# Query and key weights in eight transfers instead of two, and two input tiles loaded from ScalarE's queue

## The chip, the core and the metric

The kernel runs on one core of a Trainium2 chip. The metric is the device time of one execution in microseconds (us), as the median of several runs. Engines are named as in the profile: PE is TensorE (PEld its weight loads), DVE is VectorE, ACT is ScalarE, POOL is GpSimd, SP is SyncE, which here only issues DMAs; a name with a q (SPq, ACTq) is the engine's queue of instructions that issue or wait.

## What is computed

```python
x  = layernorm(A_x)                        # 2048 tokens x 512, bf16 (A_x: the input)
s  = mixer(x, wqkv, wo)                    # 32 heads of 16; each token attends to 8 keys, 2 apart, backwards
h  = gelu(layernorm(x) @ w1)               # 512 x 512
x1 = x + shifted(h) @ w2                   # four column groups, shifted by -1, +1, -2, +2 tokens
g  = silu(x1 + gelu(layernorm(x1) @ w3) @ w4)   # 512 x 1376, 1376 x 512
out = x + s * g
```

`mixer` takes queries, keys and values as `x @ wqkv` (512 x 1536), a softmax over the 8 keys, and ends with `@ wo`. The first thing that TensorE needs is therefore a normalised tile of x and the query part of `wqkv`.

## The kernel before

Even and odd tokens are kept apart (`p` is 0 or 1, 1024 tokens each), so that the stride of 2 becomes a band. Tokens are worked on in four chunks `c` of 512, each of four tiles `j` of 128 tokens; chunk 0 and 1 are the even tokens. x lies in `xn[p]` with tokens on partitions; `load_x` fetches it, one tile (128 KB) a transfer in chunk 0, two tiles (256 KB) in the others. `wqk_sb` holds the first 1024 columns of `wqkv`, four row blocks `dt` of 128: columns 0 to 511 are the queries (`k` 0), 512 to 1023 the keys (`k` 1).

All loads at the start are issued by SP (L118, L128, L132), in this order: x tile 0, x tile 1, the query weights (one transfer of 512 KB), x tile 2, x tile 3, the key weights (512 KB), then chunk 1 and chunk 2 (two transfers each), `w1`, and chunk 3 (two).

The work of chunk 0, from L430 on, tile by tile: `stats` (DVE, L208 and L209: mean and variance), `root` (ACT, L217: the square root of the variance), `inverse` (DVE, L220: the reciprocal), `norm` (DVE, L224: subtract and multiply in place). Tiles 0 and 1 go first; `first_columns` then transposes them on PE (L290), and the two halves of the result are copied to `xnT` by DVE (L292) and ACT (L293). Then come tiles 2 and 3 in the same way. `qk(0, 0)` (L309) multiplies the first 256 tokens by the eight blocks `nt` of `wqk_sb`: `nt` 0 to 3 are queries, 4 to 7 keys, four matmuls (`dt`) each. Within it, before `nt` 6 and `nt` 7, tiles 2 and 3 are transposed by `columns` (L264), for `qk(0, 1)` after it.

Each engine executes its instructions in the order of the source: the last lines of the kernel chain each engine's instructions one behind the other. Between engines, the framework places semaphores. In the built program, every DMA that SP or ACT issues signals its landing on one of eight semaphores, taken in turn: the DMAs are numbered in the order in which the program lists them, and SP's and ACT's count in one sequence. A DMA that takes a semaphore which an earlier one used waits, on its own queue, until that one has landed. The listing of the built program is one sequence over all engines, in the order in which the framework's scheduler dispatched them; it knows the order on each engine, not these semaphores. Its first loads stand in it so (work of POOL and PE left out):

```
SP   x tile 0            signals H0
SP   x tile 1            signals H1
SP   wqk_sb (queries)    signals H2
SP   x tile 2            signals H3
SP   x tile 3            signals H4
SP   wqk_sb (keys)       signals H5
SP   chunk 1, tiles 0,1  signals H6
SP   chunk 1, tiles 2,3  signals H7
SP   chunk 2, tiles 0,1  waits H0, signals H0
SP   chunk 2, tiles 2,3  waits H1, signals H1
DVE  stats (0,0)         waits H0
SP   w1_sb               waits H2, signals H2
DVE  stats (0,1)         waits H1
ACT  root (0,0)
ACT  root (0,1)
DVE  norm (0,0), inverse (0,1), norm (0,1)
SP   chunk 3, tiles 0,1  waits H3, signals H3
DVE  copy to xnT (L292)
SP   chunk 3, tiles 2,3  waits H4, signals H4
...
SP   store to row_dram (L249, chunk 0)  waits H5, signals H5
...
SP   store of tile 7 (last lines)       signals H5
ACT  store of tile 7, second half       signals H6
SP   store of tile 7, first half        signals H7
```

The functions that the diff touches, with the line numbers of the profile:

Of the kernel before, what the change touches and what calls it, by code (L numbers as in the profile page):

```python
# [15 lines left out]
def kernel(  # L16
# [13 lines left out]
    pe, dve, act, pool, sp = nc.tensor, nc.vector, nc.scalar, nc.gpsimd, nc.sync  # L30
    P = 128
    S = 2048
    D = 512
# [4 lines left out]
    ND = D // P  # L38
# [6 lines left out]
    TPC = CH // P  # L45
# [16 lines left out]
    xv = A_x.flatten_outer_dims().rearrange("(m two) d -> two m d", two=2)  # L62
# [16 lines left out]
    def bigt(shape, name):  # L79
        return big.tile(shape, BF16, name=name, tag="big")  # L80

    def midt(shape, name):
        return mid.tile(shape, BF16, name=name, tag="s11")

    def smt(shape, name):
        return sm4.tile(shape, BF16, name=name, tag="s4")
# [25 lines left out]
    xn = [bigt([P, M // P, D], f"xn{p}") for p in range(2)]  # L112
    wqkv_v = A_wqkv.rearrange("(dt q) n -> q dt n", q=P)

    def load_x(c, n):
        p, k = c // 2, c % 2
        for t0 in range(k * TPC, (k + 1) * TPC, n):
            sp.dma_start(  # L118
                out=xn[p][:, t0 : t0 + n, :],
                in_=xv[p, t0 * P : (t0 + n) * P, :].rearrange("(i q) d -> q i d", q=P),  # L120
            )
            yield

    wqk_sb = midt([P, ND, 2 * D], "wqk_sb")
    first = load_x(0, 1)
    for k in range(2):
        next(first), next(first)
        sp.dma_start(out=wqk_sb[:, :, k * D : (k + 1) * D], in_=wqkv_v[:, :, k * D : (k + 1) * D])  # L128
    list(load_x(1, 2))
    list(load_x(2, 2))  # L130
    w1_sb = smt([P, ND, D], "w1_sb")
    sp.dma_start(out=w1_sb, in_=B_w1.rearrange("(dt q) n -> q dt n", q=P))  # L132
    list(load_x(3, 2))

    act.preload_act_table_set("sqrt_and_others")
    ident = const.tile([P, P], BF16, name="ident")
# [17 lines left out]
    for e in range(2):  # L154
        dve.tensor_reduce(
            out=sel[:, e : e + 1], in_=ident.rearrange("p (r f) -> p r f", f=2 * DH)[:, :, DH * e : DH * e + DH],
# [43 lines left out]
    def x_tile(c, j):  # L200
        return xn[c // 2][:, (c % 2) * TPC + j, :]

    def stats(c, j, key="l1"):
        if (key, c) not in mvs:
            mvs[key, c] = small.tile([P, TPC, nc.vector.BN_AGGR_DIM], F32, name=key + "m", tag=key + "m")
            rs[key, c] = small.tile([P, TPC], F32, name=key + "r", tag=key + "r")
        st = small.tile([P, nc.vector.BN_STATS_DIM], F32, name=key + "s", tag=key + "s")
        dve.bn_stats(out=st, in_=x_tile(c, j))  # L208
        dve.bn_aggr(out=mvs[key, c][:, j, :], in_=st)  # L209
# [6 lines left out]
    def root(c, a, b):  # L216
        act.activation(rs["l1", c][:, a:b], mvs["l1", c][:, a:b, 1], AF.Sqrt, bias=eps[:, 0:1])  # L217

    def inverse(c, a, b):
        dve.reciprocal(out=rs["l1", c][:, a:b], in_=rs["l1", c][:, a:b])  # L220

    def norm(c, j, key="l1", dst=None):
        x = x_tile(c, j)
        dve.tensor_scalar(  # L224
            out=x if dst is None else dst, in0=x, scalar1=mvs[key, c][:, j, 0:1], scalar2=rs[key, c][:, j : j + 1],
            op0=ALU.subtract, op1=ALU.mult,
        )
# [201 lines left out]

    stats(0, 0)  # L430
    root(0, 0, 1)
    stats(0, 1)
    root(0, 1, 2)
    for j in range(2):
        inverse(0, j, j + 1)
        norm(0, j)
# [52 lines left out]
    for j in range(TPC):  # L489
# [12 lines left out]
        out=w4_sb[:, 0 : NF - 1, :],  # L502
        in_=B_w4[0 : (NF - 1) * P, :].rearrange("(ft q) n -> q ft n", q=P),
# [364 lines left out]
    for n in range(NN - 1):  # L868
# [56 lines left out]
        if n - 1 in final_at and n % 2 == 0 and n < NN - 3:  # L925
            p, i = final_at[n - 1]
# [88 lines left out]
```

## Time and profile before

| | |
|---|---|
| time, median of 3 runs | 198.19 us (197.81 to 198.98) |
| the profiled execution's own time | 197.92 us |
| its span, first to last instruction | 195.9 us |
| PE busy | 189.5 us (97%) |
| DVE, ACT, POOL busy | 124.1 us, 126.7 us, 62.9 us |
| mean granted TensorE clock | 0.998 |
| first matmul of `qk(0, 0)` | 6.73 us from the span's start |
| DMA traffic, first three of 40 slices (4.9 us each) | 149, 330, 270 GB/s |

The span is what the profile shows from the first to the last instruction; 2.0 us of the execution's time lie outside it. The times of instructions are counted from the span's start. A busy share is an average over the whole span; what a change at the start is worth must be read from the first ten microseconds.

### The profile page before, as it was taken

The page shows a single profiled execution, that of the slowest core. Times are in us where ns is not written, and L with a number is a line of the kernel's source. Part 1 is how long each engine was busy: PE and PEld are TensorE (multiplying, and loading weights), DVE is VectorE, ACT ScalarE, POOL GpSimd, SP SyncE. Part 2 cuts the span into 40 slices and gives each one's busy share as a digit, 9 for nine tenths or more (in the row PEclk, how much of TensorE's full clock was granted, in tenths as well). Part 3 has the DMA queues.
Part 4 walks back from the last instruction along what each step waited for, and adds up shares of the span by engine and source line. Part 5 has one row for each costly group of instructions (what it writes and reads, how often), then busy time and mean ns, then how long its engine had stood idle before and what let it go on. Part 6 is the DMA issues. An engine that isn't in the chain of part 4 may idle for free.

```text
span 195.9 us, 6180 instructions
## 1 busy us (share of the span) xinstructions
PE 189.5 (97%) x2607; PEld 100.7 (51%) x2607; DVE 124.1 (63%) x247; ACT 126.7 (65%) x140; POOL 62.9 (32%) x114
## 2 busy tenths in 40 slices
PE   7799999999999999999999999999999999999992
PEld 2688748644444444444445555555555545546551
DVE  4879885029359968200005677788778888886893
ACT  3579867836721534666558788887666666677971
POOL 4146738201301121100000623032625242469761
PEclk9999999999999999999999999999999999999999
DMA  5985265799660366350420012222233271723243
GB/s 149 330 270 137 77 144 161 141 300 357 185 155 3 107 157 162 113 107 0 155 84 0 14 25 65 76 48 67 44 97 67 56 210 27 234 39 87 70 141 109
DMA packets 36251, 23.36 MB, mean 119 GB/s; under 512 B 19680, under 2 KB 35712, under 8 KB 36224
## 3 DMA queue, kind: packets, MB, share of 16 engines
q1 hardware_dynamic: 34864, 22.11, 40.2%
q0 software_dynamic: 1216, 0.81, 2.1%
q8 instruction: 20, 0.33, 0.7%
q10 hardware_dynamic: 144, 0.07, 0.1%
q14 instruction: 7, 0.06, 0.1%
HBM read 12.41 MB, written 5.36 MB: 91 GB/s over the span
## 4 chain that ended last, share of the span: by engine, by line
PE 90%; DVE 4%; ACT 2%; DMA 1%; issue 1%; DVEq 0%
PE w_ps L542 19%; PE w_ps L406 18%; PE qk_ps L309 14%; PE v_ps L595 8%; PE w_ps L342 7%; PE w_ps L366 7%; PE wo_ps L815 5%; PE o_ps L663 5%; PE s_ps L616 3%; PE w_ps L422 1%; DMA xn<-in_A_x_dram 1%; ACT prob L627 1%; DVE prob L636 1%; PE tr_ps L264 1%; PE dt_ps L716 1%
## 5 line engine op out<-in xcount | busy, mean ns | idle before, releaser
L627 ACT ACTIVATE prob<-s_ps 128x2048 bf16<-128x2048 f32 (+1 forms) x18 | 31.9, 1780 | 17.9 <-PE s_ps L616 17.9
L542 PE MATMUL w_ps<-w_sb,h3T 128*128 128x512 bf16 (+1 forms) x176 | 40.8, 380 | 0.0
L410 ACT ACTIVATE h3T<-w_ps 128x1024 bf16<-128x1024 f32 x20 | 20.5, 1023 | 24.9 <-PE w_ps L406 24.9
L706 POOL DMA_DIRECT2D oT<-orw x38 | 19.4, 518 | 49.8 <-DVE orw L671 30.3
L406 PE MATMUL w_ps<-x1nT,w_sb 128*128 128x512 bf16 x160 | 35.0, 379 | 0.0
L309 PE MATMUL qk_ps<-xnT,wqk_sb 128*128 128x256 bf16 (+1 forms) x224 | 29.7, 288 | 0.5 <-DVE xnT L292 0.4
L542 PEld LDWEIGHTS <-h3T 128*128 128x128 bf16 (+1 forms) x176 | 17.0, 98 | 20.4
L309 PEld LDWEIGHTS <-wqk_sb 128*128 128x128 bf16 x224 | 21.5, 98 | 7.6 <-issue 0.8
L406 PEld LDWEIGHTS <-w_sb 128*128 128x128 bf16 x160 | 15.6, 98 | 19.1 <-issue 0.4
L636 DVE TENSOR_TENSOR prob<-prob,band 128x2048 bf16<-128x2048 bf16 (+1 forms) x18 | 21.3, 1183 | 2.4 <-ACT prob L627 2.3
L316 ACT ACTIVATE qT<-qk_ps,sel 128x1024 bf16<-128x1024 f32 x16 | 16.8, 1111 | 7.1 <-PE qk_ps L309 7.0
L831 POOL TENSOR_TENSOR xo<-sg,xo 128x512 bf16<-128x512 bf16 x9 | 11.7, 1305 | 21.6 <-DVE sg L826 21.6
L371 DVE TENSOR_TENSOR xn<-w_ps,xn 128x1024 bf16<-128x1024 f32 x8 | 9.7, 1212 | 13.2 <-PE w_ps L366 13.2
L815 PE MATMUL wo_ps<-wo_sb,oT 128*128 128x512 bf16 (+1 forms) x68 | 16.6, 367 | 0.1
L595 PE MATMUL v_ps<-wv_sb,xnT 128*128 128x512 bf16 x64 | 16.6, 382 | 0.0
L550 DVE TENSOR_TENSOR xn<-w_ps,xn 128x512 bf16<-128x512 f32 x15 | 10.4, 690 | 7.5 <-PE w_ps L542 7.5
L598 DVE CAST v_aug<-v_ps 128x512 bf16<-128x512 f32 x1 | 0.7, 691 | 22.5 <-ACT h3T L410 22.5
L681 ACT ACTIVATE orw<-o_ps 128x896 bf16<-128x896 f32 x16 | 14.6, 913 | 0.4 <-PE dt_ps L716 0.4
L366 PE MATMUL w_ps<-w_sb,hT 128*128 128x512 bf16 x64 | 14.3, 379 | 0.0
L342 PE MATMUL w_ps<-xn2T,w_sb 128*128 128x512 bf16 x64 | 14.3, 379 | 0.0
L213 POOL TENSOR_SCALAR l3r<-l3m 128x4 f32<-128x4 f32 x4 | 1.8, 451 | 36.9 <-DVE l3m L209 36.9
L663 PE MATMUL o_ps<-prob,v_aug 64*32 64x64 bf16 x1088 | 12.2, 196 | 0.3 <-DVE prob L636 0.2
(100 smaller groups left out, 240.1 us busy)
## 6 DMA issues: line engine op xcount, KB each, us to landing
x1n_dram<-xn SPq DMA_DIRECT2D x4, 512.0 KB
xn<-in_A_x_dram SPq DMA_DIRECT2D x6, 256.0 KB
xo<-in_A_x_dram SPq DMA_DIRECT2D x6, 256.0 KB
out_dram<-xo SPq DMA_DIRECT2D x6, 256.0 KB
orw<-rden_d SPq DMA_DIRECT2D x6, 240.0 KB
w_sb<-in_B_w_dram SPq DMA_DIRECT2D x1, 1376.0 KB
w_sb<-in_B_w_dram SPq DMA_DIRECT2D x1, 1280.0 KB
wqk_sb<-in_A_wqkv_dram SPq DMA_DIRECT2D x2, 512.0 KB
```

Source lines behind the costliest of these rows:

```text
L309: pe.matmul(pt[:, b, :], lhsT=wqk_sb[:, dt, nt * P : (nt + 1) * P], rhs=xnT[p][:, dt, ms], start=(dt == 0), stop=(dt == ND - 1),)
L342: pe.matmul(pt[:, b, :], lhsT=w1_sb[:, dt, g * P : (g + 1) * P], rhs=xn2T[:, dt, :], start=(dt == 0), stop=(dt == ND - 1),)
L366: pe.matmul(pt[:, j, :], lhsT=w2_src(p, g, m0), rhs=w2_sb[:, g, :], start=(g == 0), stop=(g == ND - 1),)
L406: pe.matmul(pt[:, b, :], lhsT=w3_sb[:, dt, ft * P : (ft + 1) * P], rhs=x1nT[:, dt, :], start=(dt == 0), stop=(dt == ND - 1),)
L410: act.activation(h3_tile(c)[:, 2 * a : 2 * a + 2, :], pt, AF.Gelu_apprx_tanh)
L542: pe.matmul(pt, lhsT=h3[c][:fs, ft, jj * P : (jj + 1) * P], rhs=w4_sb[:fs, ft, :], start=(ft == 0), stop=(ft == NF - 1 and t < NN - 2),)
L595: pe.matmul(vp, lhsT=xnT[p][:, dt, k0 : k0 + P], rhs=wv_sb[:, dt, :], start=first, stop=last)
L627: act.activation(pr[:, rs_], t[:, rs_], AF.Exp, scale=SCALE)
L636: dve.tensor_tensor(out=w, in0=w, in1=b.unsqueeze(1).to_broadcast([P, m, KB]), op=ALU.min)
L663: pe.matmul(op[32 * cg : 32 * cg + 32, s, g * KB : (g + 1) * KB], lhsT=va[KB * s : KB * s + KB, dt * 8 + h, :], rhs=pr[KB * s : KB * s + K ...
L706: queues[hh % len(queues)].dma_start(out=oT[p][DH * hh : DH * (hh + 1), :, q0 : q0 + nq], in_=w[32 * cg : 32 * cg + DH, ND * jj : ND * jj ...
L815: pe.matmul(pt, lhsT=oT[p][:, dt, i * P : (i + 1) * P], rhs=wo_sb[:, dt, cs], start=(dt == 0), stop=(dt == ND - 1),)
```

## The change

The two transfers of `wqk_sb` become eight, one for each half `k` and row block `dt`: 128 rows of 512 columns, 128 KB each. They follow x tiles 0 and 1 directly on SP's queue. x tiles 2 and 3 leave SP's queue: ACT issues them, the one behind `root(0, 0)`, the other behind `root(0, 1)`. The order of SP's other loads stays. The number of transfers at the start goes from 13 to 19. `load_x` becomes a plain function with a queue as argument.

```diff
-    def load_x(c, n):
-        p, k = c // 2, c % 2
-        for t0 in range(k * TPC, (k + 1) * TPC, n):
-            sp.dma_start(...)
-            yield
+    def load_x(c, j, n=1, queue=sp):
+        p, t0 = c // 2, c % 2 * TPC + j
+        queue.dma_start(
+            out=xn[p][:, t0 : t0 + n, :], in_=xv[p, t0 * P : (t0 + n) * P, :].rearrange("(i q) d -> q i d", q=P)
+        )
 
     wqk_sb = midt([P, ND, 2 * D], "wqk_sb")
-    first = load_x(0, 1)
+    for j in range(2):
+        load_x(0, j)
     for k in range(2):
-        next(first), next(first)
-        sp.dma_start(out=wqk_sb[:, :, k * D : (k + 1) * D], in_=wqkv_v[:, :, k * D : (k + 1) * D])
-    list(load_x(1, 2))
-    list(load_x(2, 2))
+        for dt in range(ND):
+            sp.dma_start(out=wqk_sb[:, dt, k * D : (k + 1) * D], in_=wqkv_v[:, dt, k * D : (k + 1) * D])
+    for c in (1, 2):
+        for j in (0, 2):
+            load_x(c, j, 2)
     w1_sb = smt([P, ND, D], "w1_sb")
     sp.dma_start(out=w1_sb, in_=B_w1.rearrange("(dt q) n -> q dt n", q=P))
-    list(load_x(3, 2))
+    for j in (0, 2):
+        load_x(3, j, 2)
...
     stats(0, 0)
     root(0, 0, 1)
+    load_x(0, 2, 1, act)
     stats(0, 1)
     root(0, 1, 2)
+    load_x(0, 3, 1, act)
     for j in range(2):
         inverse(0, j, j + 1)
         norm(0, j)
     first_columns()
```

More of the change, by code (lines that the diff above doesn't have):

```diff
@@ L113 @@
     wqkv_v = A_wqkv.rearrange("(dt q) n -> q dt n", q=P)
-    def load_x(c, n):
-        p, k = c // 2, c % 2
-        for t0 in range(k * TPC, (k + 1) * TPC, n):
[L118 to L121, printed above, removed]
-            yield
+    def load_x(c, j, n=1, queue=sp):
[3 more added lines that the diff above has]
+        )
     wqk_sb = midt([P, ND, 2 * D], "wqk_sb")
-    first = load_x(0, 1)
+    for j in range(2):
+        load_x(0, j)
     for k in range(2):
-        next(first), next(first)
-        sp.dma_start(out=wqk_sb[:, :, k * D : (k + 1) * D], in_=wqkv_v[:, :, k * D : (k + 1) * D])
-    list(load_x(1, 2))
-    list(load_x(2, 2))
+        for dt in range(ND):
[3 more added lines that the diff above has]
+            load_x(c, j, 2)
     w1_sb = smt([P, ND, D], "w1_sb")
     sp.dma_start(out=w1_sb, in_=B_w1.rearrange("(dt q) n -> q dt n", q=P))
-    list(load_x(3, 2))
+    for j in (0, 2):
+        load_x(3, j, 2)
     act.preload_act_table_set("sqrt_and_others")
```

## The prediction

> **What bounds the kernel now.** The page first: PE is busy for 189.5 of 195.9 us, and the chain that ended last is 90% PE.
>
> ```profile
> PE 90%; DVE 4%; ACT 2%; DMA 1%; issue 1%; DVEq 0%
> ```
>
> So whatever moves the first matmul moves the end by as much: behind it PE works without a pause that a late start could fill. The change touches the first 10 us only, so I read the chain there in order of time (start, length, what).
>
> ```profile
> 0.80 2.33 DMA xn<-in_A_x_dram
> ...
> 3.15 0.70 DVE l1s L208
> ...
> 4.06 0.59 DVE l1s L208
> ...
> 5.46 0.43 DVE xn L224
> ...
> 5.93 0.30 PE tr_ps L290 x2
> ...
> 6.25 0.44 DVE xnT L292
> ...
> 6.73 2.94 PE qk_ps L309 x24
> ```
>
> x tile 0 lands, DVE takes the statistics of tiles 0 and 1, normalises both, PE transposes, DVE copies, and at 6.73 the first `qk` matmul starts. Neither the weights nor x tiles 2 and 3 are on this chain. The waits of the first 30 us show what the weights do cost:
>
> ```profile
> PEld L309 <- DMA wqk_sb<-in_A_wqkv_dram: 0.2, 1, 0.2
> ```
>
> One wait, that of `nt` 4 for the keys (landed at 8.58 by the trace's landing events). In matmul starts it is less: matmul 17 starts 0.195 us behind matmul 16, where the others keep 0.109. The loss is 0.09 us. That is all that earlier weights can win on PE.
>
> ACT's timeline shows the place of the two roots, and that ACT has room around them:
>
> ```profile
> 4.10 0.29 ACT L217 ACTIVATE l1r<-l1m,eps 128x1 f32<-128x1 f32 x1 [2.02 <-DVE l1m L209]
> 4.89 0.29 ACT L217 ACTIVATE l1r<-l1m,eps 128x1 f32<-128x1 f32 x1 [0.50 <-DVE l1r L220]
> 6.37 0.60 ACT L293 ACTIVATE xnT<-tr_ps 128x512 bf16<-128x512 bf16 x1 [1.18 <-PE tr_ps L290]
> ```
>
> The second root is as good as on the chain: it ends at 5.18, its reciprocal starts at 5.26 beside the end of the first norm, and `norm(0, 1)` at 5.46 needs both. If the root is late, all is late after 0.03 us.
>
> Last, SP's waits in the first 15 us:
>
> ```profile
> SPq L249 <- DMA wqk_sb<-in_A_wqkv_dram: 0.5, 1, 0.5
> ```
>
> The store of L249 reads `r2t` and has nothing to do with `wqk_sb`. It is the 14th DMA, the key weights are the 6th: fourteen less eight. This is the ring of eight semaphores at work, and it does hold a queue. `w1` (the 11th) says the same: the 3rd landed at 5.771, `w1` was issued at 5.788.
>
> **The change, part by part.** *Eight pieces on SP.* Issues stand in SP's timeline:
>
> ```profile
> 0.80 0.88 SPq L118 DMA_DIRECT2D xn<-in_A_x_dram  x2
> 1.72 0.43 SPq L128 DMA_DIRECT2D wqk_sb<-in_A_wqkv_dram  x1
> 2.19 0.98 SPq L118 DMA_DIRECT2D xn<-in_A_x_dram  x2
> 3.21 0.43 SPq L128 DMA_DIRECT2D wqk_sb<-in_A_wqkv_dram  x1
> ```
>
> The first seven starts are 0.45 to 0.55 us apart, whatever the size; I take 0.48. The pieces then start at 1.72, 2.20, 2.68, 3.16 (queries) and 3.64, 4.12, 4.60, 5.08 (keys), and chunk 1 at 5.56 instead of 3.69. A 128 KB transfer with nothing ahead of it landed 2.33 and 2.24 us after its issue (x tiles 0 and 1); one behind a 512 KB transfer took 3.9 (tile 2). At 128 KB each 0.48 us (273 GB/s) the pieces stay below the 330 GB/s of the page's second slice, so nothing piles up: 2.2, between 2.0 and 2.4. The queries are there at 5.36, before 6.73; the last keys at 7.28, before the 8.54 at which `nt` 4 is due. Gain 0.09. Chunk 1, 1.9 us later, is needed at 9.36 and would land by 8.6 (2.2, 0.4 for its second 128 KB, 0.4 for what ACT adds); SP's other loads have microseconds to spare, and SP ends its loads near 10, before L249 at 12.29.
>
> The Trainium skill, "DMA: Bandwidth & Descriptors", under "Rules for kernel authors", advises against such cuts: many small transfers should be made one large one. By its fit in "Anatomy of one DMA" (2.0 us and bytes over 436 GB/s, given for another path) a piece takes an estimated 2.3 us, and the sum below would grow by 0.1.
>
> *Two issues on ACT.* The only DMA that ACT issues in the trace:
>
> ```profile
> 192.90 0.39 ACTq L857 DMA_DIRECT2D out_dram<-slots  x1
> ```
>
> If ACT's first issue starts when the first root ends (4.39) and takes 0.39 to 0.51 (SP's rows), it ends between 4.78 and 4.90: 0 to 0.05 us on the second root. The other one lies in the idle time before L293.
>
> *The wait that these issues bring.* This is the costly part. x tile 2 takes a semaphore of the ring, and which one depends on how many DMAs are listed ahead of it. In the listing of before, `w1` stands before `root(0, 0)`, and the first load of chunk 3 behind `root(0, 1)`. With two loads taken out of SP's order ahead of them, both stand earlier if anything. So 15 DMAs are ahead of x tile 2 (two tiles, eight pieces, four of chunks 1 and 2, `w1`), perhaps 16. As the 16th it waits for the 8th to land, the second piece of the keys; as the 17th for the 9th, the third piece. x tile 3 as the 18th waits for the 10th, the last piece. No data are involved.
>
> The 8th is issued at 4.12 and lands at 6.32. ACT executes in order, so behind its wait stand `root(0, 1)`, x tile 3 and L293; for the root waits DVE (`inverse(0, 1)`, `norm(0, 1)`), for that PE. The second root then starts at 6.32 + 0.02 (as `w1` behind its release) + 0.41 (issue) + 0.04 (gap) = 6.79 instead of 4.89: 1.90, less the slack of 0.03, is **1.87 us** on the chain.
>
> x tile 3 may issue at 7.28 and ends at 7.7; L293, now due at 8.24, isn't held. But the tiles come late: tile 2, issued at 6.34, shares the DMA engines with the 256 KB loads of chunks 1 and 2; between 2.3 (alone) and 3.9 (behind 512 KB) I take 2.6, so 8.9 and for tile 3 9.9. DVE wants tile 3 at 7.41 + 1.87 = 9.28 and needs 1.89 us from there to the end of its norm (7.41 to 9.30): 11.8. PE wants it at 10.06 + 1.8 = 11.9, and tile 2, whose norm ends 1.37 after tile 3 is taken, at 9.40 + 1.8 = 11.2 against 11.3. Cost 0 to 0.5; I take **0.2**.
>
> Sum: 1.87 + 0.2 - 0.09 = 1.98 us. Against the profiled execution (197.92) that is 199.90, against the median (198.19; the profile lies 0.27 below) 200.17. Forecast 200.0. With the low value of each term (pieces 0.45 apart, landing in 2.0, issue 0.39, tiles in time) the cost is 1.4; as the 17th, with 0.50, 2.4, 0.51 and 0.5, it is 3.2. So 199.4 to 201.2 for this case.
>
> **The rivals.** *No wait decides: not slower.* If the ring doesn't hold ACT's queue, or x tile 2 is the 12th DMA or earlier, its predecessor has landed by 4.4 and ACT issues between the roots. Then tile 2 lands at 6.7 to 6.9, 0.1 to 0.3 after DVE asks (6.59), which PE doesn't feel: the norm of tile 2 ends at 8.78, its transposes start at 9.40. What stays is the 0.09: 198.1. For it: no ACT issue in this trace waits on the ring. Against it: the listing gives ACT's last DMA its number between two of SP's.
>
> *A shorter wait.* If SP's pieces are dispatched slower than I read from the listing, x tile 2 is the 13th to 15th and waits for a landing at 4.88, 5.36 or 5.84: 0.4 to 1.4 us, 198.6 to 199.6. Against it: the scheduler put `w1`, with 2.5 MB of loads ahead of it, before the root, and now there are 2.25 MB ahead.
>
> *The clock falls.* Between the warm-up matmuls, which end at 4.8, and `qk`, now at 8.6, PE has only eight transposes, 0.9 us in all; before, the pause was 1.9 us. In this trace the matmuls of L147 are 0.427 us apart until 3.65 and 0.217 from 4.0, so a cold PE takes twice the time. Warming took 2.9 us here; so much `qk` work at half speed adds some 1.5 us: 201.5. The Trainium skill, "TensorE: Matmul & The Clock Gate", "The HAM clock gate", says that the half rate returns after an idle window of about 3.4 us that runs freely; no pause here is that long and empty, and the trace has no drop at 1.9.
>
> **How the numbers follow.** The long wait 0.70; no wait 0.14; a shorter wait 0.08; the clock 0.07; rest 0.01. About 0.5% (1 us) is what a measurement of this kernel can tell. Faster by more than that needs a mechanism that I don't see: 0.01. Same: no wait and half of the shorter waits, 0.18. Slower: the rest, 0.81. The range 198.1 to 201.2 holds nearly all of the long and shorter waits and some of no wait.
>
> **What would show it.** In the changed kernel's ACT timeline `root(0, 1)` starts near 6.8, with an ACTq issue right ahead of it that starts within 0.05 us of the landing of a key piece; the first `qk` matmul at 8.6; DVE's wait for the late tiles 0 to 0.6 us; no wait for `wqk_sb`; the first chunk 1 issue near 5.6. Wrong if ACT issues x tile 2 at 4.4, or if the second root stays at 4.9.

## The result and the profile after

The changed kernel takes 206.1 us (median of 6 runs, 204.87 to 208.15), the kernel before 198.29 us: a ratio of 1.037 (95% interval 1.032 to 1.042). The ratios, here and below, leave out single slow runs, over 1.5% above the fastest of their kernel (208.15 here, 202.91 in wait_alone, 207.39 in keep_warm), which medians and ranges still contain: the medians differ by 7.8 us, the ratio stands for 7.3. The forecast was 200.0 us, in a range of 199.4 to 201.2: the sign was right, the size about four times too small. The profiled execution took 204.87 us, its span is 202.9 us; against the 195.9 us of before that is 7.0.

The page's share of the chain that ended last, by engine, and its line on the granted clock:

```profile
PEclk9889999999999999999999999999999999999999
...
PE 72%; DMA 12%; DVE 5%; ACT 3%; SPq 3%; issue 2%; ACTq 0%; DVEq 0%
```

PE has fallen from 90% to 72%, DMA risen from 1% to 12%, and the clock has a dent in the second and third slice. The waits of the first 30 us (engine and line, what was waited for, total, times, longest):

```profile
DVE l1s L208 <- DMA xn<-in_A_x_dram: 6.2, 3, 3.1
...
ACT l1r L217 <- DMA wqk_sb<-in_A_wqkv_dram: 3.2, 1, 3.2
PE tr_ps L264 <- DVE xn L224: 3.2, 1, 3.2
```

The second line is the wait that the prediction named: a square root that waits for a weight transfer. But the first is twice as long: DVE's statistics wait for x tiles (1.4 us of it for tile 0, as before; the rest for tiles 2 and 3). The timeline shows both in their places (start, length, engine, line, what; in brackets the idle time before it and what ended it):

```profile
4.05 0.29 ACT L217 ACTIVATE l1r<-l1m,eps 128x1 f32<-128x1 f32 x1 [1.97 <-DVE l1m L209]
...
7.08 0.38 ACTq L117 DMA_DIRECT2D xn<-in_A_x_dram  x1
7.50 0.29 ACT L217 ACTIVATE l1r<-l1m,eps 128x1 f32<-128x1 f32 x1 [3.16 <-DMA wqk_sb<-in_A_wqkv_dram]
...
8.31 0.33 ACTq L117 DMA_DIRECT2D xn<-in_A_x_dram  x1
...
12.42 0.69 DVE L208 BATCH_NORM_STATS2 l1s<-xn 128x6 f32<-128x512 bf16 x1 [3.07 <-DMA xn<-in_A_x_dram]
...
15.09 0.69 DVE L208 BATCH_NORM_STATS2 l1s<-xn 128x6 f32<-128x512 bf16 x1 [1.76 <-DMA xn<-in_A_x_dram]
```

ACT stood from 4.34 to 7.08 ahead of its first issue: the second key piece, the 8th DMA, landed at 7.059. The second root began at 7.50 instead of 4.89. So far this is the forecast, larger. Then the tiles: issued at 7.08 and 8.31, they were there at 12.40 and 15.07. DVE took tile 3 at 15.09; before it was at 7.41:

```profile
7.41 0.66 DVE L208 BATCH_NORM_STATS2 l1s<-xn 128x6 f32<-128x512 bf16 x1
```

The chain of the changed kernel in order of time says which of the two, the root or the tiles, sets the end:

```profile
4.57 3.73 DMA wqk_sb<-in_A_wqkv_dram
...
8.31 6.75 DMA xn<-in_A_x_dram
...
15.09 0.70 DVE l1s L208
...
16.60 0.41 DVE xn L224
...
18.19 2.89 PE qk_ps L309 x24
```

The third key piece lands at 8.29, this releases the issue of tile 3 (the 17th DMA, eight after the 9th), its load takes 6.75 us, and `qk` on the second 256 tokens starts at 18.19. In the kernel before, the same piece of the chain stands at 11.07:

```profile
11.07 2.89 PE qk_ps L309 x24
```

These 7.1 us are the loss: ACT's instructions lie 7.1 us later at that point and between 6.8 and 7.3 us later from there to the end. The second root isn't on this chain at all.

### The profile page after: what moved, and what is told of

Same layout as the page of the kernel before. It is cut to its first block, busy times and chain, and to the rows that moved or that the text cites. A ratio compares the mean times of both kernels' runs of the same rounds, so it can differ in the third digit from the quotient of the medians.

```text
span 202.9 us, 6162 instructions
## 1 busy us (share of the span) xinstructions
PE 189.7 (93%) x2582; PEld 101.3 (50%) x2607; DVE 124.2 (61%) x247; ACT 126.5 (62%) x140; POOL 62.5 (31%) x114
## 4 chain that ended last, share of the span: by engine, by line
PE 72%; DMA 12%; DVE 5%; ACT 3%; SPq 3%; issue 2%; ACTq 0%; DVEq 0%
PE w_ps L406 17%; PE w_ps L544 12%; PE qk_ps L309 12%; PE w_ps L366 7%; PE w_ps L342 7%; PE v_ps L597 6%; PE o_ps L665 4%; DMA xn<-in_A_x_dram 3%; PE wo_ps L817 3%; DMA slots<-in_A_x_dram 2%; DMA oT<-orw 2%; PE s_ps L618 2%; DMA wqk_sb<-in_A_wqkv_dram 2%; DMA rden_d<-rb 1%; ACT orw L683 1%
## 5 line engine op out<-in xcount | busy, mean ns | idle before, releaser
L309 PE MATMUL qk_ps<-xnT,wqk_sb 128*128 128x256 bf16 (+1 forms) x223 | 30.6, 295 | 0.5 <-DMA xn<-in_A_x_dram 0.3
L309 PEld LDWEIGHTS <-wqk_sb 128*128 128x128 bf16 x224 | 22.2, 100 | 8.0 <-DMA xn<-in_A_x_dram 0.5
L638 DVE TENSOR_TENSOR prob<-prob,band 128x2048 bf16<-128x2048 bf16 (+1 forms) x18 | 21.2, 1179 | 2.6 <-ACT prob L629 2.5
L597 PE MATMUL v_ps<-wv_sb,xnT 128*128 128x512 bf16 x49 | 15.8, 383 | 0.8
L208 DVE BATCH_NORM_STATS2 l1s<-xn 128x6 f32<-128x512 bf16 x16 | 10.8, 675 | 6.2 <-DMA xn<-in_A_x_dram 6.2
```

What stands on the lines that cost most here:

```text
L309: pe.matmul(pt[:, b, :], lhsT=wqk_sb[:, dt, nt * P : (nt + 1) * P], rhs=xnT[p][:, dt, ms], start=(dt == 0), stop=(dt == ND - 1),)
L597: pe.matmul(vp, lhsT=xnT[p][:, dt, k0 : k0 + P], rhs=wv_sb[:, dt, :], start=first, stop=last)
L638: dve.tensor_tensor(out=w, in0=w, in1=b.unsqueeze(1).to_broadcast([P, m, KB]), op=ALU.min)
```

## The experiments

Five theories were put against each other. **A**: the two loads on ACT's queue are the loss. It has two forms, A1 (they wait in the ring of semaphores) and A2 (they land late, because a load lands only when what was issued before it, on whatever queue, has landed). **B**: many small transfers drain slower than few large ones. **C**: the second root behind the wait, the prediction's main term. **D**: ACT's queue is slow by itself. **E**: the fallen clock. Diffs are against the changed kernel unless the text says otherwise. Lines of helpers shift by a few between kernels.

### pieces_only: eight pieces, no load on ACT

```diff
-    for j in range(2):
-        load_x(0, j)
     for k in range(2):
+        load_x(0, 2 * k)
+        load_x(0, 2 * k + 1)
         for dt in range(ND):
             sp.dma_start(out=wqk_sb[:, dt, k * D : (k + 1) * D], in_=wqkv_v[:, dt, k * D : (k + 1) * D])
...
-    load_x(0, 2, 1, act)
...
-    load_x(0, 3, 1, act)
```

> The eight pieces alone; x tiles 2 and 3 back on SP's queue between the query and the key pieces, as before. Theory A (the loss comes from the two loads on ACT's queue: issued late behind the ring of semaphores, then landing very late): no loss, 198.0 to 198.6 us. Theory B (small transfers are slow: in the changed kernel the last key piece landed 3.6 us after its issue instead of the 2.2 that I used): the last key piece, issued near 6.0, lands at 9.6, a microsecond after nt 4 wants it, and x tile 3 near 7.7: 199 to 199.8 us with a PE wait for wqk_sb of about 0.6 us.

Measured: 199.47 us, ratio 1.0044 (1.0019 to 1.0068). So most of the loss is in the two loads that the change moved to ACT, but the pieces aren't free, as B has it. From its waits of the first 20 us:

```profile
PEld L309 <- DMA wqk_sb<-in_A_wqkv_dram: 1.3, 2, 1.0
...
PE qk_ps L309 <- DMA wqk_sb<-in_A_wqkv_dram: 0.8, 1, 0.8
```

The matmuls themselves stop once, for 0.8 us. The last key piece landed at 10.09; in the kernel before the keys were complete at 8.58, behind the same 1.5 MB.

### act_only: two loads on ACT, weights in two transfers

```diff
     for k in range(2):
-        for dt in range(ND):
-            sp.dma_start(out=wqk_sb[:, dt, k * D : (k + 1) * D], in_=wqkv_v[:, dt, k * D : (k + 1) * D])
+        sp.dma_start(out=wqk_sb[:, :, k * D : (k + 1) * D], in_=wqkv_v[:, :, k * D : (k + 1) * D])
```

> The two loads on ACT's queue alone; the weights stay two transfers of 512 KB. x tile 2 is now the 10th DMA and waits for the 2nd (landed at 3.5), so it issues at 4.4; x tile 3 is the 12th and waits for the 4th, the key weights. Theory A1 (what costs is the wait in the ring): tile 2 lands by 7, the second root stays at 4.9, first qk matmul at 6.7; tile 3 is held until the keys land, 7 to 8, and L293 with it; 199.5 to 201 us. Theory A2 (what costs is that a load on ACT's queue lands late while SP's queue is full, 5.3 and 6.8 us in the changed kernel): tile 2 lands near 9.7 and tile 3 near 14: 203 to 205 us.

Measured: 204.68 us, ratio 1.032 (1.028 to 1.036). Its ACT timeline:

```profile
3.89 0.37 ACTq L117 DMA_DIRECT2D xn<-in_A_x_dram  x1
4.68 0.29 ACT L216 ACTIVATE l1r<-l1m,eps 128x1 f32<-128x1 f32 x1 [0.50 <-DVE l1r L219]
7.65 0.33 ACTq L117 DMA_DIRECT2D xn<-in_A_x_dram  x1
8.03 0.60 ACT L292 ACTIVATE xnT<-tr_ps 128x512 bf16<-128x512 bf16 x1 [3.05 <-DMA wqk_sb<-in_A_wqkv_dram]
10.81 0.29 ACT L216 ACTIVATE l1r<-l1m,eps 128x1 f32<-128x1 f32 x1 [2.19 <-DVE l1m L208]
14.16 0.29 ACT L216 ACTIVATE l1r<-l1m,eps 128x1 f32<-128x1 f32 x1 [3.06 <-DVE l1r L219]
```

The first issue has no wait and the second root is at 4.68, as early as can be. Still tile 2, issued at 3.89, landed at 9.85, 5.95 us later. Tile 3 did wait in the ring (for the keys, 7.63) and landed at 13.20. The roots at 10.81 and 14.16 belong to tiles 2 and 3. Tile 2 shows A2 without any wait. Tile 3, which sets the end, has both: held back until 7.65 (A1), then 5.55 us from issue to landing (A2).

### roots_first: both loads on ACT behind the second root

```diff
     root(0, 0, 1)
-    load_x(0, 2, 1, act)
     stats(0, 1)
     root(0, 1, 2)
+    load_x(0, 2, 1, act)
     load_x(0, 3, 1, act)
```

> The changed kernel with both loads of ACT behind the second root, so no root waits in ACT's queue; x tile 2 still waits for the 8th DMA, x tile 3 is the 18th and waits for the 10th. Theory A2 (the landing of tile 3 sets the start of qk on the second 256 tokens): as late as in the changed kernel or later, 205 to 207 us, with the second root at 4.9. Theory C (my prediction's main term: the root behind the wait): 2.6 us less than the changed kernel, 202.3 to 203.5 us.

Measured: 206.67 us, ratio 1.040 (1.033 to 1.047). Its ACT timeline:

```profile
4.78 0.29 ACT L217 ACTIVATE l1r<-l1m,eps 128x1 f32<-128x1 f32 x1 [0.50 <-DVE l1r L220]
7.10 2.21 ACTq L117 DMA_DIRECT2D xn<-in_A_x_dram  x2
9.37 0.60 ACT L293 ACTIVATE xnT<-tr_ps 128x512 bf16<-128x512 bf16 x1 [4.30 <-DMA wqk_sb<-in_A_wqkv_dram]
```

The second root stood at 4.78, and nothing was won: tile 3, now the 18th DMA, issued at 8.98 and landed at 15.23. This alone doesn't rule out C, because the wait only moved: it now holds ACT's half of the copy to `xnT` (L293), and all but two of the first 24 `qk` matmuls start at 10.02 or later. sp_late, below, has no wait on ACT at all.

### act_early: the loads on ACT at the very start

```diff
     act.preload_act_table_set("sqrt_and_others")
+    load_x(0, 2, 1, act)
+    load_x(0, 3, 1, act)
```

The two later calls are gone.

> The eight pieces, and x tiles 2 and 3 on ACT's queue behind its first table load (issued near 2.1 and 2.5), as the 4th and 6th DMA: no wait in the ring. Theory A1 and A2 alike: the tiles land by 5.5, before DVE asks at 6.6; 198.0 to 198.5 us. Theory D (ACT's queue is slow whatever is on SP's): they land at 7.4 to 9, and the time is 199 to 201 us. Theory B: the last key piece lands at 8.7 or later, PE waits for it up to 0.3 us: 198.3 to 198.7 us.

Measured: 198.99 us, ratio 1.0026 (0.9996 to 1.0056). ACT issued at 0.82 and 1.26, already during the table load; the tiles landed at 3.52 and 4.23, 2.7 and 3.0 us after the issue. D falls: the same queue, used when little is issued ahead, is quick. The median is 0.3 us over B's range, and its interval includes no loss at all.

### hold_back: the changed kernel with SP's later loads held back

```diff
+    gap_dram = dram.tile([1, 2], F32, name="gap_dram")
...
-    for c in (1, 2):
-        for j in (0, 2):
-            load_x(c, j, 2)
...
-    for j in (2, 3):
-        stats(0, j)
-        root(0, j, j + 1)
+    stats(0, 2)
+    sp.dma_start(out=gap_dram, in_=mvs["l1", 0][0:1, 2, :])
+    for c in (1, 2):
+        for j in (0, 2):
+            load_x(c, j, 2)
...
+    root(0, 2, 3)
+    stats(0, 3)
+    root(0, 3, 4)
```

> The changed kernel, with the loads of chunks 1 to 3 and of w1 held back on SP until the statistics of x tile 2 are there (a store of two numbers from them, ahead of these loads on SP's queue). ACT's loads are now the 11th and 12th DMA and wait for the first two pieces, landed by 4.8: no wait to speak of, and nothing but weight pieces ahead of them. Theory A2 in its sharp form (a load on ACT's queue lands as late as one that SP issues at the same moment: all bytes issued before it come first): tile 2 lands with the third and last key pieces, 7.3 to 8.4, tile 3 8.6 to 9.2; 199 to 200.5 us, chunk 1 being late too. Theory D (ACT's queue is slow by itself): 5.5 us from issue to landing as in the changed kernel, tile 2 at 10, tile 3 at 10.7 or later, 201.5 us or more.

Measured: 201.4 us, ratio 1.015 (1.011 to 1.018). The ring had no wait, issues stood at 4.10 and 4.69, and the tiles landed at 8.58 and 9.32: each a little ahead of the SP piece issued next to it (4.08, landed at 8.76; 4.55, landed at 9.51). That is A2 in its sharp form. The time was a microsecond over the expected range, and the chain says why: the loads held back were late.

```profile
4.10 4.48 DMA xn<-in_A_x_dram
...
9.88 2.78 DMA xn<-in_A_x_dram
...
12.69 0.70 DVE l1s L202
```

### sp_late: no load on ACT, tiles 2 and 3 late on SP

```diff
             load_x(c, j, 2)
+    load_x(0, 2)
     w1_sb = smt([P, ND, D], "w1_sb")
     sp.dma_start(out=w1_sb, in_=B_w1.rearrange("(dt q) n -> q dt n", q=P))
+    load_x(0, 3)
...
-    load_x(0, 2, 1, act)
...
-    load_x(0, 3, 1, act)
```

> The changed kernel without any load on ACT's queue: x tiles 2 and 3 go back to SP, but to the places in the order of issue that they have in the changed kernel, behind chunks 1 and 2 and around w1 (issued near 7.5 and 8.5). No root waits. Theory A2 (a load lands when all bytes issued before it have landed, whatever queue it is on; that is the whole loss): tile 2 lands near 13, tile 3 near 15, the second 256 tokens' first qk matmul near 18.2, and 204.5 to 206.5 us, as the changed kernel. Rival D (ACT's queue is served worse than SP's): 200 to 203 us. Rival C (the root's wait is a part of the loss): 2 us or more faster than the changed kernel.

Measured: 206.99 us, ratio 1.044 (1.039 to 1.048). Without ACT's queue, without a wait of ACT, the whole loss is back, though the first `qk` matmul starts on time, at 6.61. So neither D nor C is the loss of the changed kernel. The ACT timeline has the second root at 4.76:

```profile
4.76 0.29 ACT L219 ACTIVATE l1r<-l1m,eps 128x1 f32<-128x1 f32 x1 [0.50 <-DVE l1r L222]
```

Its chain in order of time has the same load as that of the changed kernel:

```profile
8.52 7.27 DMA xn<-in_A_x_dram
...
17.28 0.61 PE tr_ps L266 x4
17.89 0.85 PE qk_ps L311 x4
```

Tile 3 landed at 15.79. The median lies 0.5 over the expected range; PE's clock was at half from 14.4 to 21.2 here, and the four matmuls of the last line take 0.85 us where they take 0.44 at full clock.

### wait_alone and wait_warm: the root's wait by itself

Against the kernel before: chunk 3's loads go to ACT, behind the two roots.

```diff
-    list(load_x(3, 2))
...
+    late = load_x(3, 2, act)
     root(0, 0, 1)
+    next(late)
     stats(0, 1)
     root(0, 1, 2)
+    next(late)
```

> The kernel before, with nothing changed but the two loads of chunk 3, needed only 15 us later: ACT issues them behind its first two roots. The first is the 12th DMA and waits for the 4th (x tile 2, 6.1 us). So a root waits in ACT's queue, and no tile that is needed comes late. Theory C (my prediction's main term, alone): the second root starts near 6.55 instead of 4.89, the first qk matmul near 8.4, and 1.6 us are lost: 199.6 to 200.0 us. Rival: the loss is hidden by the slack of tiles 2 and 3 or by PE's later work, 198.2 to 198.8 us.

Measured: 201.2 us, ratio 1.011 (1.004 to 1.017). The second root stood at 6.95, behind an issue released by tile 2 at 6.46, and the first `qk` matmul at 8.86 instead of 6.73: 2.1 us, so the chain that the prediction built is real. The time was over the expected range, and it scattered with the clock: 199.24 (mean clock 1.00), 201.04 and 201.37 (0.99), 202.9 (0.98). Two stages of the profiled execution (201.37), cut at the clock's edges (length, then busy time and instructions of PE, PEld, DVE, ACT and POOL; the last three numbers are clock, DMA share and GB/s):

```profile
7.78:11.20 3.42, 2.95 (x16) 2.11 (x17) 2.79 (x10) 1.19 (x3) 0.13 (x1) 0.50 1.04 348
11.20:14.00 2.80, 2.80 (x30) 2.49 (x29) 1.33 (x4) 2.07 (x2) 1.56 (x4) 1.00 0.92 295
```

For 3.4 us the clock was at half. The same kernel with eight matmuls of ones in the pause (`warm(n)` issues n of the matmuls that warm PE up at the start):

```diff
         for j in range(2):
+            if j == 1:
+                warm(8)
             for dt in range(ND):
                 pe.transpose(pts[dt // 2][:, dt % 2, j, :], x_tile(0, j)[:, dt * P : (dt + 1) * P], ident[:])
```

> wait_alone with 8 matmuls of ones ahead of the transposes of tile 1, so that PE isn't idle while the second root waits. If the scatter of wait_alone (199.2 to 202.9 us) comes from the clock that falls in the pause: granted clock 0.998 or more in every run, and the pure price of the root's wait, 2.0 us by the second root (4.89 to 6.95 in the profile): 199.3 to 200.4 us. Rival: scatter and median stay as they were, 201.2 us.

Measured: 199.81 us, ratio 1.0075 (1.0051 to 1.0100), ten runs from 199.10 to 200.39, all at 0.997 or more. The 24 matmuls of the first group show the clock's price in the two chains, 3.91 us against 2.84. In wait_alone:

```profile
8.86 3.91 PE qk_ps L308 x24
```

and in wait_warm:

```profile
8.59 2.84 PE qk_ps L314 x24
```

So the root's wait alone costs 1.5 us. The runs of wait_alone at a mean clock of 0.99 lie another 1.2 to 1.6 higher.

### keep_warm: the changed kernel with PE busy in its pauses

The same `warm`, ten ahead of tile 1's transposes and 18 ahead of tile 2's.

> The changed kernel, with PE multiplying ones by ones in its pauses: 10 such matmuls of the warm-up's kind ahead of the transposes of tile 1, 18 ahead of those of tile 2 (2.2 and 3.9 us at full clock). Theory E (the fallen clock is a part of the loss and of its scatter): granted clock 0.996 or more, time 204.3 to 205.0 us in every run, against 204.9 to 208.2 of the changed kernel. Theory A2 alone (PE waits for tile 3 anyway, so half speed before it costs nothing): the median stays near 206 us, and the scatter too.

Measured: 205.02 us, ratio 1.032 (1.027 to 1.036), runs from 204.1 to 207.4. The clock stayed at 0.996 or more, but the profiled execution had the same span (203.0) and started the second `qk` at 18.14, with tile 3 landed at 15.01. So in the changed kernel's profiled execution the clock cost nothing, because its half-speed matmuls end before tile 3 is there. Whether it makes up part of the changed kernel's scatter stays open. Its runs at a mean clock of 0.992 took 204.87 and 204.88, those at 0.979 to 0.982 took 205.26 to 207.40, which points that way; but E expected 205.0 or less in every run of keep_warm, and the intervals of the two ratios overlap.

### four_pieces and act_early_two: the size of the transfers

four_pieces is pieces_only with two row blocks a transfer (256 KB); act_early_two is act_early with the two transfers of before.

> The weights in four transfers of 256 KB, x tiles on SP's queue in the order of before; to be read beside pieces_only (eight of 128 KB, last key piece landed at 10.1) and the kernel before (two of 512 KB, 8.6). Theory B (the more transfers, the slower they drain): the last key lands near 9.2, 198.4 to 198.9 us. Rival (the loss of pieces_only is only in its order of issue): as before or a little faster, 198.0 to 198.2 us.

Measured: 199.44 us, ratio 1.0051 (1.0025 to 1.0077). The last key piece landed at 9.21, between 8.58 (two transfers) and 10.09 (eight), in order of their number as B expects. By itself that is weak: in wait_alone and wait_warm, whose first seven loads are those of the kernel before, the keys landed at 8.78 and 9.39. What the DMA engines moved between 5.0 and 8.4 us is clearer: 290 to 358 GB/s in the five kernels with two weight transfers, 270 with four, 206 to 252 in the seven with eight. The time is that of eight pieces, more than expected, though in the profile `qk` on the second 256 tokens starts only 0.4 us later than before (1.2 in pieces_only). So B gives the slower transfers, but not the whole loss of four_pieces, which stays open.

> The weights in two transfers of 512 KB as before, x tiles 2 and 3 issued by ACT at the very start, beside x tiles 0 and 1; to be read beside act_early (the same with eight pieces: 198.99 us, last key piece landed at 9.2). Theory B (pieces drain slower): the keys land by 8.6 as before, and the residue of act_early goes; x tile 0 lands 0.2 us later for the company: 198.2 to 198.6 us. Rival (the early company is the whole residue): 198.8 to 199.2 us.

Measured: 198.52 us, ratio 1.0021 (0.9986 to 1.0056). The keys were complete only at 9.20, not at 8.6, and x tile 0 landed at 3.53 instead of 3.13 for the company of ACT's loads. Beside act_early the difference (198.52 and 198.99) is within the intervals: what these two leave over the kernel before, if anything, can't be told apart.

No version beat the kernel before. By its trace none of these could by much: its DVE never waits for tiles 2 and 3, and the keys cost it 0.09 us.

## Why the prediction was right and wrong

**The wait: right.** x tile 2 was the 16th DMA and waited for the 8th, its issue came 0.02 us behind that landing, the second root stood behind it, and SP's first load of chunk 1 went out at 5.51 (forecast 5.56). Tile 3 was the 17th and waited for the 9th, not the 18th behind the 10th. wait_warm gives the price of such a wait alone: 1.5 us for a root that is 1.9 late (6.79 instead of 4.89), less than the 1.87 at which the prediction put the same delay.

**The landing of the pieces: mis-sized.** The prediction took 2.2 us from issue to landing for each piece, because x tiles 0 and 1 had 2.2 to 2.3. In the changed kernel the four query pieces took 2.5 to 3.2, the key pieces that the two waits hang on (the 8th and the 9th DMA) 2.97 and 3.73. "Nothing piles up" was wrong: it compared 273 GB/s with the 330 of the second slice, which transfers of up to 512 KB had reached; with pieces the same slice moved 244. So the second root came at 7.50 and not at 6.79, and tile 3 was issued at 8.31 and not at 7.28.

The rule that advised against the cuts (the Trainium skill, "DMA: Bandwidth & Descriptors", "Rules for kernel authors") was the better guide here: eight pieces and four both measured 0.4% to 0.5% slower than two transfers.

**The landing of tiles 2 and 3: the step that failed.** The prediction put 2.6 us, from 2.3 (alone) and 3.9 (behind one 512 KB transfer), and a cost of 0.2 us (0.5 at most). They took 5.3 and 6.75 us. Tile 3 was to land at 9.9 and landed at 15.07: of these 5.2 us, 1.0 is its late issue and 4.15 the time from issue to landing. They are about what the forecast of 1.98 us lacks to the 7.0 of the spans, and the late root, the main term of the sum, is hidden behind them.

What stood wrong was the choice of the row. The trace of before had the right one: SP's loads issued between 3.7 and 7.5 us landed 5.6 to 7.4 us after their issue. The prediction treated ACT's queue as a way past them, and its rival without a wait did so too: act_only's tile 2, issued at 3.89 without a wait, landed at 9.85, not at 6.7 to 6.9. The table puts each load on ACT's queue beside the SP load issued next to it (landing events of the traces; "outstanding": bytes issued before it on both queues and not yet landed):

| kernel | ACT's load: issued, landed (us) | us | outstanding KB | SP's neighbour: issued, landed |
|---|---|---|---|---|
| act_early, tile 2 | 0.82, 3.52 | 2.7 | 128 | 0.80, 3.33 |
| hold_back, tile 2 | 4.10, 8.58 | 4.5 | 640 | 4.08, 8.76 |
| hold_back, tile 3 | 4.69, 9.32 | 4.6 | 768 | 4.55, 9.51 |
| changed, tile 2 | 7.08, 12.40 | 5.3 | 1280 | 7.01, 13.28 |
| act_only, tile 2 | 3.89, 9.85 | 6.0 | 1792 | 3.81, 10.41 |
| changed, tile 3 | 8.31, 15.07 | 6.8 | 1792 | 8.67, 15.90 |
| act_only, tile 3 | 7.65, 13.20 | 5.5 | 1920 | 8.39, 14.49 |

In these rows a load on either queue lands about when its turn comes in the common order of issue, in the changed kernel 0.8 to 0.9 us ahead of its neighbour. The bytes outstanding set the time only roughly: the last row, from a kernel with large weight transfers, is quicker than the one above it with more outstanding. The most that ACT's queue gained is in wait_alone and wait_warm: the first of its two 256 KB loads landed 1.6 and 1.8 us ahead of `w1` (512 KB), which SP had issued 0.3 to 0.4 us earlier. In sp_late nearly the same turn on SP's queue (tile 3 issued at 8.52) gave the same loss.

The Trainium skill, "DMA: Bandwidth & Descriptors", "Queues, rings and completion order", says that each DMA engine goes round the queues that have work, packet by packet. From that one would estimate that 128 KB on a queue of their own get half of the engines and are through in twice their own time. Of the bytes that moved while ACT's packets did, half were indeed ACT's in act_early (128 KB beside 139 of SP's) and in wait_alone (512 beside 567), but not in the changed kernel (tile 2: 128 beside 438) or in act_only (128 beside 536). On the same page, under "Issuing engines are not separate DMA queues", the Trainium skill says that issuing from several engines saves only the time that it takes to initiate the DMA; sp_late agrees (206.99 us without ACT's queue, 206.1 with it). Part of the delay lies ahead of the first packet: ACT's first packet moved 1.3 us after the issue in act_early, 2.5 in the changed kernel, 3.6 in act_only and 3.9 in wait_alone. What holds it there no run shows.

**The clock: right as a mechanism, wrong in its chance.** A fall of the clock got 0.07. It fell in the profiled execution (half speed from 8.4 to 11.8), and all six runs have a mean clock of 0.992 or less, where the kernel before has 0.996 or more in the runs beside the experiments. It fell in three of the four runs of wait_alone too, where PE's pause is 2 us longer than before. The pauses held four transposes ahead of the fall, so they were not the empty window that the prediction asked for: PE was busy for 0.74 us of the 3.4 before the fall in the changed kernel, for 1.03 in wait_alone. In the changed kernel's profile the fall was covered by the wait for tile 3, in wait_alone's runs at 0.99 it cost 1.2 to 1.6 us.

**No wait for the keys: right, and worth nothing.** The wait of 0.09 us was gone as forecast, since all of PE's work was late.

## What to carry to other kernels

In these runs a second DMA queue was no way past the loads that the first one had already issued, or one of 1.8 us at most: count the bytes issued and not yet landed at the moment of the issue, and take the time to landing from a load of the trace that was issued under a like backlog. Put a load that is needed soon ahead in the order of issue, not on another queue behind compute. And where a framework hands out a small ring of DMA semaphores, more and smaller transfers move every later load closer to a wait, which stops whatever compute stands behind the issue on that engine.

## What the runs showed of the hardware that was not expected

- ACT's DMA issues run beside its table load: in act_early they started at 0.82 and 1.26, while the load ran from 0.79 to 2.07. An issue also starts beside the root ahead of it, not at its end as the prediction had it: both at 3.89 in act_only.
- Transfers of 128 KB kept the DMA engines less busy than larger ones: 206 GB/s between 5.0 and 8.4 us in pieces_only, 314 in the kernel before. In pieces_only 12 transfers (1.5 MB) landed between 2.98 and 10.09 us; the same bytes in 6 transfers landed between 3.13 and 8.58.
- A pause of PE with four transposes in it was enough for the clock to halve for 3.4 us (wait_alone, changed kernel); it was at half for 6.8 us in sp_late, with a pause of 7.75 us, and for 10.2 in roots_first. In wait_warm eight matmuls of ones in the pause kept the mean clock at 0.997 or more in ten of ten runs.
